# Paired 64 KB loads into a fixed buffer in a memory-bound decode kernel

## The chip, the cores and the metric

The kernel runs on one core of one Trainium2 chip. The metric is device time in microseconds. A difference is called resolved when its 95% interval excludes zero, and "the same" when it stays within 2%.

## The reference, cut to what matters

```
x: [1, 1, 1024]     k_cache, v_cache: [1, 4, 65536, 128]  (67 MB each, bf16)
q = (x @ wq) as 32 heads of 128; each of the 4 KV heads serves 8 query heads
p = softmax(q @ k.T / sqrt(128));  o = p @ v;  a = o @ wo
b = gated MLP of x through w_in [1024, 3584] and w_out [1792, 1024]
out = sigmoid(sum(x * gate_w)) * a + (1 - that) * b
```

One token attends over two caches of 67 MB. With the weights, 162 MB come from HBM and 2 KB go back.

## The kernel before

Every large input goes through one ring of four buffers of 32 KB per partition (a pool with four buffers in turn, called "regions" below where the changed kernel has them in one tile). One sync queue issues all large loads in program order; a load waits until the last reader of its buffer is done.

```python
CT, NKV = 128, 4
def load(src, shape, name):
    t = kv.tile([P, CT * P], BF16, name=name, tag="kv")
    ...
    ins = nc.sync.dma_start(out=v, in_=src)
def load_kv(src, g, j, name):                 # 4 MB: 128 partitions x 32 KB
    k0 = j * CT * P
    return load(src[0, g, k0:k0 + CT * P, :].rearrange("(p c) d -> p (c d)", c=CT),
                (CT * DH,), name)

win_t = [load(... half i of w_in ...) for i in range(2)]
wq_t  = [load(... half i of wq ...) for i in range(2)]
# ... q ...
for g in range(G):                            # 4 KV heads
    for j in range(NT):                       # 4 tiles of 16384 keys
        k_tile(g, j, load_kv(A_k_cache, g, j, "kn"))
        if j == NT - 1:
            stats(g)
        if g > 0:
            v_tile(g - 1, j, load_kv(A_v_cache, g - 1, j, "vt"))
        elif j == NT - 1:
            project(load(... w_out ...), FC, uT, 0, first=True)
    if g > 0:
        head_out(g - 1)
# ... last V tiles, wo in six pieces, then:
nc.scalar.copy(out=out_sb[:], in_=out_ps[:])
nc.scalar.dma_start(out=..., in_=out_sb[::B, :])        # four partitions
```

`k_tile` transposes a K tile on VectorE (DVE) and multiplies it on TensorE (PE); a K buffer is free after its fourth transpose. `v_tile` is PE alone. `stats(g)` is the maximum and the exponentials of head g.

Of the kernel before, what the change touches and what calls it, by code (L numbers as in the profile page):

```python
# [8 lines left out]
BF16 = mybir.dt.bfloat16  # L9
# [5 lines left out]
P = 128  # L15
CT = 128
NKV = 4
B = 32
# [5 lines left out]
WO_SPLIT = ((16,), (8, 4, 2, 1, 1))  # L24
# [3 lines left out]
def kernel(  # L28
# [15 lines left out]
    nc = tc.nc  # L44

    _, _, D = A_x.shape
    _, G, S, DH = A_k_cache.shape
    HD = A_wq.shape[1]
    H = HD // DH
    REP = H // G  # L50
    F = B_w_in.shape[1]
    FH = F // 2
    KC = D // P
    FC = FH // P
    OC = HD // P
    QD = P // H
    NT = S // (P * CT)
# [8 lines left out]
    const = ctx.enter_context(tc.tile_pool(name="const", bufs=1))  # L66
    wk = ctx.enter_context(tc.tile_pool(name="wk", bufs=2))
    big = ctx.enter_context(tc.tile_pool(name="big", bufs=1))
    kv = ctx.enter_context(tc.tile_pool(name="kv", bufs=NKV))
    ktp = ctx.enter_context(tc.tile_pool(name="ktp", bufs=3))  # L70
    scp = ctx.enter_context(tc.tile_pool(name="scp", bufs=NT + 1))
    ptp = ctx.enter_context(tc.tile_pool(name="ptp", bufs=NT + 2))
# [7 lines left out]
    def same_weights(ins):  # L80
        held.add(ins.ins.name)
# [33 lines left out]

    nc.at_finalize(start_first_load)

    def load(src, shape, name):
        t = kv.tile([P, CT * P], BF16, name=name, tag="kv")
        n = 1  # L120
        for s in shape:
            n *= s
        v = t[:, :n]
        if len(shape) == 2:
            v = v.rearrange("p (a b) -> p a b", b=shape[1])
        ins = nc.sync.dma_start(out=v, in_=src)
        if not first_load:
            first_load.append(ins.ins.name)
        return v

    def load_kv(src, g, j, name):
        k0 = j * CT * P
        return load(src[0, g, k0:k0 + CT * P, :].rearrange("(p c) d -> p (c d)", c=CT),
                    (CT * DH,), name)


    xg8 = const.tile([KC, 2, P], BF16, name="xg8")
# [5 lines left out]

    KH = KC // 2
    win_view = B_w_in.rearrange("(p c) n -> p c n", c=KC)
    win_t = [load(win_view[:, i * KH:(i + 1) * KH, :], (KH, F), "win_t") for i in range(2)]
    wq_view = A_wq.rearrange("(p c) n -> p c n", c=KC)
    wq_t = [load(wq_view[:, i * KH:(i + 1) * KH, :], (KH, HD), "wq_t") for i in range(2)]


    row = const.tile([P, P], FP32, name="row")
# [41 lines left out]
    for t in range(2):  # L193
        nc.vector.tensor_tensor(
            out=xm[:, t], in0=xb_ps[:, t * P:(t + 1) * P].rearrange("p (i c) -> p c i", c=KC),
# [51 lines left out]
    for hf in range(2):  # L247
        nc.vector.tensor_tensor(  # L248
            out=zm[:, hf], in0=z_ps[:, hf * HN:hf * HN + ZN].rearrange("p (j c) -> p j c", c=FC),
# [3 lines left out]
                            in_=zm.rearrange("p h j c -> p h c j"), axis=AX.X, op=ALU.add)  # L253
# [44 lines left out]
    for k in range(NHB):  # L298
        xs = slice(k * NX // NHB, (k + 1) * NX // NHB)
        nc.vector.tensor_tensor(  # L300
            out=qm[:, xs], in0=q_ps[:, k * HN:(k + 1) * HN].rearrange("p (x j e) -> p x j e",
                                                                   j=B, e=2),
# [6 lines left out]
        out=q4[:], in0=q1[:].rearrange("p x e -> p (x e)").unsqueeze(1).to_broadcast(  # L309
            [P, NB, NX * 2]),  # L310
# [7 lines left out]
    for g in range(G):  # L318
        k, t0 = g * T2 // NB, g * T2 % NB
        nc.vector.tensor_copy(out=qs[:, g].rearrange("p b (t h) -> p b t h", t=T2),  # L320
                              in_=qv[:, k, t0:t0 + T2].rearrange("p t h b -> p b t h"))

    def build_w(g):
        for v in range(VC):
            nc.vector.tensor_tensor(
                out=wt[g % 2][:, v, :, :, v, :],
                in0=qs[:, g].unsqueeze(2).to_broadcast([P, BP, NB, REP]),
                in1=own_n[:].unsqueeze(1).unsqueeze(3).to_broadcast([P, BP, NB, REP]),
                op=ALU.mult)

    oa = const.tile([P, OC], BF16, name="oa")
# [3 lines left out]
    def k_tile(g, j, kn):  # L335
        kb = kn.bitcast(I32)
        n = CC * DH // 2
        s_ps = pss.tile([P, 2 * HN], FP32, name="s_ps", tag="s")
        for v in range(VC):
            kt = ktp.tile([P, CC * DH], BF16, name="kt")  # L340
            nc.vector.transpose(out=kt[:].bitcast(I32), in_=kb[:, v * n:(v + 1) * n])  # L341
            while late:
                nc.vector.reduce_max(**late.pop())  # L343
            kx = kt[:].rearrange("p (c h k e) -> p h e c k", h=2, k=B, e=2)
            for b in range(BP):
                for k in range(2):
                    ins = nc.tensor.matmul(  # L347
                        s_ps[:, k * HN:(k + 1) * HN],
                        lhsT=wt[g % 2][:, v, b].rearrange("p a v h -> p (a v h)"),
                        rhs=kx[:, b // 2, b % 2, k * CC // 2:(k + 1) * CC // 2, :],  # L350
                        start=(v == 0 and b == 0), stop=(v == VC - 1 and b == BP - 1),
                        skip_group_check=True)
                    if k > 0:
                        same_weights(ins)
        if j == 0:
            mxs[g] = wk.tile([P, NT], FP32, name="mx")
        sct[g, j] = scp.tile([P, CC * B], BF16, name="sc")
        nc.scalar.copy(out=sct[g, j][:], in_=s_ps[:])  # L358
        late.append(dict(out=mxs[g][:, j:j + 1], in_=sct[g, j][:], axis=AX.X))
# [26 lines left out]
    def v_tile(g, j, vt):  # L386
        if j == 0:
            o_ps[g] = pso.tile([P, 2, VC * DH], FP32, name="o_ps")
        vx = vt.rearrange("p (v c d) -> p c v d", v=VC, d=DH)
        for u in range(CC // 2):  # L390
            hs = slice(u % 2 * P // 2, (u % 2 + 1) * P // 2)
            for e in range(2):
                ins = nc.tensor.matmul(  # L393
                    o_ps[g][hs, e, :],
                    lhsT=ptt[g, j][:, 2 * u:2 * u + 2, :].rearrange("p c x -> p (c x)"),
                    rhs=vx[:, 2 * u + e], start=(j == 0 and u < 2),
                    stop=(j == NT - 1 and u >= CC // 2 - 2), skip_group_check=True)
                if e > 0:
                    same_weights(ins)
# [29 lines left out]
    NO = D // NB  # L429
    out_ps = psl.tile([P, NO], FP32, name="out_ps")  # L430

    def project(w, n, vec, c0, first=False, last=False):
        for c in range(n):
            for t in range(NB):
                nc.tensor.matmul(  # L435
                    out_ps[t * B:(t + 1) * B, :],
                    lhsT=vec[:, c0 + c:c0 + c + 1].to_broadcast([P, B]),
                    rhs=w[:, c, t * NO:(t + 1) * NO],
                    start=(first and c == 0), stop=(last and c == n - 1),
                    skip_group_check=True)  # L440
# [2 lines left out]
    build_w(0)  # L443
    for g in range(G):
        for j in range(NT):
            k_tile(g, j, load_kv(A_k_cache, g, j, "kn"))
            if j == 1 and g + 1 < G:
                build_w(g + 1)
            if j == NT - 1:
                stats(g)  # L450
            if g > 0:
                v_tile(g - 1, j, load_kv(A_v_cache, g - 1, j, "vt"))
            elif j == NT - 1:
                project(load(B_w_out.rearrange("(p c) n -> p c n", c=FC), (FC, D), "wout_t"),
                        FC, uT, 0, first=True)
        if g > 0:
            head_out(g - 1)
    for j in range(NT):
        v_tile(G - 1, j, load_kv(A_v_cache, G - 1, j, "vt"))
    head_out(G - 1)  # L460


    wo_view = A_wo.rearrange("(p c) n -> p c n", c=OC)
    c0 = 0
    for split in WO_SPLIT:
        t = kv.tile([P, CT * P], BF16, name="wo_t", tag="kv")
        t = t[:].rearrange("p (c n) -> p c n", n=D)
        b = c0
        for n in split:
            nc.sync.dma_start(out=t[:, c0 - b:c0 - b + n, :], in_=wo_view[:, c0:c0 + n, :])  # L470
            project(t[:, c0 - b:c0 - b + n, :], n, oa, c0, last=(c0 + n == OC))
            c0 += n
    out_sb = const.tile([P, NO], BF16, name="out_sb")
    nc.scalar.copy(out=out_sb[:], in_=out_ps[:])
    nc.scalar.dma_start(out=out.rearrange("o t (q n) -> (o t q) n", n=NO), in_=out_sb[::B, :])

    last = {}
    for ins in list(nc.cur_bb.bb.instructions):
# [36 lines left out]
```

## Time and profile before

| | before |
|---|---|
| time, median | 385.04 us (384.94 to 385.17, 3 runs) |
| span of the profiled run | 383.4 us |
| PE, DVE busy | 62%, 57% |
| load queue's share of 16 DMA engines | 98.6% |

Three lines of the profile's page, of the kernel before: TensorE's busy time, the DMA row of the 40-slice view (9 is 90% or more of a slice), and the load queue's row of the DMA table (packets, MB, share).

```profile
...
PE 237.4 (62%) x1372; PEld 58.5 (15%) x796; DVE 218.3 (57%) x211; ACT 39.6 (10%) x55; POOL 4.4 (1%) x10
...
DMA  9999999999999999999999999999999999999994
...
q1 hardware_dynamic: 6192, 162.01, 98.6%
...
```

Nothing but the DMA engines is full. In the packet records an engine takes packets one after another: their durations add up to 378.1 us per engine, in a window of 378.5 us from the first packet to the last. So the time is first of all the sum of the packets' durations, and then whatever time the queue was empty.

This is the sync queue's timeline of the kernel before around the change from head 0 to head 1 (start, duration, what was issued):

```profile
...
start us, us, engine line op out<-in xcount [idle before <-releaser]
59.26 0.33 SPq L126 DMA_DIRECT2D wout_t<-in_B_w_out_dram  x1
70.54 0.33 SPq L126 DMA_DIRECT2D kn<-in_A_k_cache_dram  x1
81.39 0.33 SPq L126 DMA_DIRECT2D vt<-in_A_v_cache_dram  x1
92.24 0.33 SPq L126 DMA_DIRECT2D kn<-in_A_k_cache_dram  x1
101.17 0.33 SPq L126 DMA_DIRECT2D vt<-in_A_v_cache_dram  x1
...
```

Each load waits for a buffer. The K load at 70.54 reuses K tile 1's buffer, the V load at 81.39 K tile 2's, the K load at 92.24 K tile 3's.

The end of the program, kernel before: the last copy and the output store.

```profile
...
380.47 0.37 ACT L474 CAST out_sb<-out_ps 128x256 bf16<-128x256 f32 x1 [47.63 <-PE out_ps L435]
380.88 0.61 ACTq L475 DMA_DIRECT2D out_dram<-out_sb  x1
```

From the start of the copy to the end of the span (383.375 us) are 2.91 us.

### The profile page before, as it was taken

To read this page: it belongs to the slowest core of one execution; us is meant where nothing else is said; L and a number is where in the kernel's file an instruction comes from. 1 tells how busy PE (TensorE), PEld (TensorE's weight loads), DVE (VectorE), ACT (ScalarE), POOL (GpSimd) and SP (SyncE) were. 2 spreads that over 40 slices of the span, in tenths; PEclk is the share of its full clock that TensorE was granted. 3 is DMA by queue.
4 is the path that set the end of the run, shared out by engine and by line. 5 is a ranking of instruction groups with operands and counts; after the bars stand their busy time and mean duration, and the time that the engine had idled before them with its cause. 6 is when DMAs were issued, how large, how long until landed. Compare 5 with 4: busy or idle time off the path is not lost.

```text
span 383.4 us, 2650 instructions
## 1 busy us (share of the span) xinstructions
PE 237.4 (62%) x1372; PEld 58.5 (15%) x796; DVE 218.3 (57%) x211; ACT 39.6 (10%) x55; POOL 4.4 (1%) x10
## 2 busy tenths in 40 slices
PE   0433357675378749465699393665983937786553
PEld 0110011111212102011121020111210201221132
DVE  4241478996697373758964645679655546720040
ACT  1010001111601101014011010140110101400000
POOL 4000000000000000000000000000000000000000
PEclk9956659999779959698699697975997978668886
DMA  9999999999999999999999999999999999999994
GB/s 374 436 427 427 422 432 431 438 435 437 426 434 424 422 431 434 438 434 431 429 431 427 427 431 433 438 427 427 434 429 424 431 435 434 432 427 428 431 417 193
DMA packets 6248, 162.18 MB, mean 423 GB/s; under 512 B 728, under 2 KB 732, under 8 KB 1116
## 3 DMA queue, kind: packets, MB, share of 16 engines
q1 hardware_dynamic: 6192, 162.01, 98.6%
q8 instruction: 8, 0.13, 0.1%
q14 instruction: 4, 0.03, 0.0%
q10 hardware_dynamic: 44, 0.01, 0.0%
HBM read 162.01 MB, written 0.00 MB: 423 GB/s over the span
## 4 chain that ended last, share of the span: by engine, by line
DMA 63%; DVE 19%; PE 10%; issue 5%; ACT 1%; SPq 0%; ACTq 0%; DVEq 0%
DMA kn<-in_A_k_cache_dram 53%; DVE kt L341 16%; DMA wo_t<-in_A_wo_dram 8%; PE s_ps L347 6%; DMA wb<-in_B_b_sp_dram 3%; PE o_ps L393 3%; DVE pt L383 1%; ACT sc L358 1%; PE z_ps L234 1%; DVE o_sb L408 0%; SPq L470 0%; ACT sc L380 0%; DVE mx L362 0%; DVE om L404 0%; DVE mx L343 0%
## 5 line engine op out<-in xcount | busy, mean ns | idle before, releaser
L347 PE MATMUL s_ps<-kt,wt 128*128 128x512 bf16 x512 | 138.1, 425 | 73.5 <-DVE kt L341 73.4
L341 DVE STREAM_TRANSPOSE kt<-kn 128x2048 int32<-128x2048 int32 x64 | 143.3, 2283 | 68.1 <-DMA kn<-in_A_k_cache_dram 65.2
L393 PE MATMUL o_ps<-vt,pt 128*64 128x512 bf16 x512 | 69.5, 433 | 7.9 <-DMA vt<-in_A_v_cache_dram 7.9
L347 PEld LDWEIGHTS <-wt 128*128 128x128 bf16 x256 | 26.9, 105 | 185.6 <-issue 121.5
L358 ACT CAST sc<-s_ps 128x1024 bf16<-128x1024 f32 x16 | 16.2, 1013 | 254.6 <-PE s_ps L347 254.6
L393 PEld LDWEIGHTS <-pt 128*64 128x64 bf16 x256 | 17.3, 124 | 57.2 <-issue 55.7
L383 DVE STREAM_TRANSPOSE pt<-sc 128x1024 bf16<-128x1024 bf16 x16 | 18.6, 1217 | 6.8 <-ACT sc L380 6.8
L404 DVE TENSOR_TENSOR om<-o_ps,own 128x1024 f32<-128x1024 f32 x4 | 4.8, 1195 | 26.4 <-PE o_ps L393 26.4
L380 ACT ACTIVATE sc<-sc,nb 128x1024 bf16<-128x1024 bf16 x16 | 18.2, 1136 | 9.7 <-DVE nb L376 9.7
L343 DVE TENSOR_REDUCE mx<-sc 128x1 f32<-128x1024 bf16 x12 | 14.3, 1188 | 1.1 <-ACT sc L358 1.0
L362 DVE TENSOR_REDUCE mx<-sc 128x1 f32<-128x1024 bf16 x4 | 4.9, 1220 | 12.1 <-ACT sc L358 12.1
L234 PE MATMUL q_ps<-wq_t,xT 128*32 128x512 bf16 x64 | 7.0, 617 | 7.5 <-DMA wq_t<-in_A_wq_dram 7.5
L414 PE MATMUL om_ps<-o_sb,hsel 128*32 128x128 f32 x8 | 2.1, 353 | 13.9 <-DVE o_sb L408 13.9
L435 PE MATMUL out_ps<-wo_t,oa 128*32 128x256 bf16 x128 | 7.0, 375 | 4.2 <-DMA wo_t<-in_A_wo_dram 2.8
L234 PE MATMUL z_ps<-win_t,xT 128*32 128x448 bf16 x64 | 6.2, 566 | 4.0 <-DMA win_t<-in_B_w_in_dram 4.0
L300 DVE TENSOR_TENSOR rowt<-q_ps,own_b 128x512 f32<-128x512 f32 x2 | 1.3, 686 | 12.4 <-PE q_ps L234 12.4
L408 DVE TENSOR_REDUCE o_sb<-om 128x128 f32<-128x1024 f32 x4 | 7.5, 1872 | 0.1
L366 PE MATMUL mt_ps<-ident_f,m 128*1 128x128 f32 x4 | 1.2, 295 | 10.2 <-DVE m L364 10.2
L248 DVE TENSOR_TENSOR rowt<-z_ps,own_b 128x448 f32<-128x448 f32 x2 | 1.2, 620 | 8.6 <-PE z_ps L234 8.6
L190 PE MATMUL xb_ps<-xg,spread 8*128 8x256 bf16 x1 | 0.4, 365 | 9.1 <-DMA xg<-in_gate_w_dram 9.1
L234 PEld LDWEIGHTS <-xT 128*32 128x32 bf16 x64 | 3.0, 138 | 19.2 <-issue 19.2
L435 PEld LDWEIGHTS <-oa 128*32 128x32 bf16 x128 | 4.5, 126 | 6.8 <-issue 4.1
(88 smaller groups left out, 56.7 us busy)
## 6 DMA issues: line engine op xcount, KB each, us to landing
kn<-in_A_k_cache_dram SPq DMA_DIRECT2D x16, 4096.0 KB, 27.2
vt<-in_A_v_cache_dram SPq DMA_DIRECT2D x16, 4096.0 KB, 32.4
wq_t<-in_A_wq_dram SPq DMA_DIRECT2D x2, 4096.0 KB, 28.2
win_t<-in_B_w_in_dram SPq DMA_DIRECT2D x2, 3584.0 KB, 15.0
wo_t<-in_A_wo_dram SPq DMA_DIRECT2D x1, 4096.0 KB, 25.9
wout_t<-in_B_w_out_dram SPq DMA_DIRECT2D x1, 3584.0 KB
wo_t<-in_A_wo_dram SPq DMA_DIRECT2D x1, 2048.0 KB
wo_t<-in_A_wo_dram SPq DMA_DIRECT2D x1, 1024.0 KB
```

Source lines behind the costliest of these rows:

```text
L234: ins = nc.tensor.matmul(ps[t * B:(t + 1) * B, k * HN:k * HN + n], lhsT=xT[:, i * KH + c:i * KH + c + 1].to_broadcast([P, B]), rhs=w[:, c, ...
L341: nc.vector.transpose(out=kt[:].bitcast(I32), in_=kb[:, v * n:(v + 1) * n])
L343: nc.vector.reduce_max(**late.pop())
L347: ins = nc.tensor.matmul(s_ps[:, k * HN:(k + 1) * HN], lhsT=wt[g % 2][:, v, b].rearrange("p a v h -> p (a v h)"), rhs=kx[:, b // 2, b % 2, ...
L358: nc.scalar.copy(out=sct[g, j][:], in_=s_ps[:])
L362: nc.vector.reduce_max(**late.pop())
L380: nc.scalar.activation(out=sct[g, j][:], in_=sct[g, j][:], func=ACT.Exp, scale=SCALE, bias=nb[:, 0:1], accum_out=lss[g][:, j:j + 1])
L383: nc.vector.transpose(out=ptt[g, j][:].rearrange("p c x -> p (c x)"), in_=sct[g, j][:])
L393: ins = nc.tensor.matmul(o_ps[g][hs, e, :], lhsT=ptt[g, j][:, 2 * u:2 * u + 2, :].rearrange("p c x -> p (c x)"), rhs=vx[:, 2 * u + e], sta ...
L404: nc.vector.tensor_tensor(out=om8[:], in0=o_ps[g][:].rearrange("p e (v d) -> p (e v) d", d=DH), in1=own_8[:].unsqueeze(2).to_broadcast([P, ...
L408: nc.vector.tensor_reduce(out=o_sb[:], in_=om8[:].rearrange("p x d -> p d x"), axis=AX.X, op=ALU.add)
L435: nc.tensor.matmul(out_ps[t * B:(t + 1) * B, :], lhsT=vec[:, c0 + c:c0 + c + 1].to_broadcast([P, B]), rhs=w[:, c, t * NO:(t + 1) * NO], st ...
```

## The change

The intent: larger rows (64 KB per partition) for the V tiles and wq, hence half as many packets; fixed places for all tiles so that two neighbouring regions can take a pair; an output store split over two queues.

```diff
-    kv = ctx.enter_context(tc.tile_pool(name="kv", bufs=NKV))
+    kv = big.tile([P, NKV * CT * P], BF16, name="kv")
-    def load_kv(src, g, j, name):
-        k0 = j * CT * P
-        return load(src[0, g, k0:k0 + CT * P, :].rearrange("(p c) d -> p (c d)", c=CT),
-                    (CT * DH,), name)
+    def load_kv(src, g, j, at, n=1):
+        k0, m = j * CT * P, n * CT
+        v = load(src[0, g, k0:k0 + m * P, :].rearrange("(p c) d -> p (c d)", c=m),
+                 (m * DH,), at)
+        return [v[:, i * CT * DH:(i + 1) * CT * DH] for i in range(n)]
...
-    win_t = [load(..., "win_t") for i in range(2)]
+    win_t = [load(..., 2 + i) for i in range(2)]
-    wq_t = [load(... half i ...) for i in range(2)]
+    wq_a = load(wq_view, (KC, HD), 0)
...
-            k_tile(g, j, load_kv(A_k_cache, g, j, "kn"))
+            k_tile(g, j, load_kv(A_k_cache, g, j, (j + 2) % NKV if g == 0 else j % 2)[0])
...
-            if g > 0:
-                v_tile(g - 1, j, load_kv(A_v_cache, g - 1, j, "vt"))
+            if g > 0 and j % 2 == 1:
+                for i, vt in enumerate(load_kv(A_v_cache, g - 1, j - 1, 2, 2)):
+                    v_tile(g - 1, j - 1 + i, vt)
...  (w_out goes to region 2; the last V tiles are one pair and two singles; wo as before)
-    nc.scalar.dma_start(out=..., in_=out_sb[::B, :])
+    for i, queue in enumerate((nc.scalar, nc.sync)):
+        p0 = (2 * i + 1) * B - 1
+        queue.dma_start(out=out_rows[2 * i:2 * i + 2, :], in_=out_sb[p0:p0 + 2, :])
```

So head 0's K tiles 0 to 3 go to regions 2, 3, 0, 1; from head 1 on, K tiles alternate between regions 0 and 1 and V pairs use regions 2 and 3.

More of the change, by code (lines that the diff above doesn't have):

```diff
@@ L116, with load @@
     nc.at_finalize(start_first_load)
-    def load(src, shape, name):
-        t = kv.tile([P, CT * P], BF16, name=name, tag="kv")
+    kv = big.tile([P, NKV * CT * P], BF16, name="kv")
+    def load(src, shape, at):
         n = 1
@@ L122, in load @@
             n *= s
-        v = t[:, :n]
+        v = kv[:, int(at * CT * P):int(at * CT * P) + n]
         if len(shape) == 2:
@@ L145 @@
     win_view = B_w_in.rearrange("(p c) n -> p c n", c=KC)
-    win_t = [load(win_view[:, i * KH:(i + 1) * KH, :], (KH, F), "win_t") for i in range(2)]
+    win_t = [load(win_view[:, i * KH:(i + 1) * KH, :], (KH, F), 2 + i) for i in range(2)]
     wq_view = A_wq.rearrange("(p c) n -> p c n", c=KC)
-    wq_t = [load(wq_view[:, i * KH:(i + 1) * KH, :], (KH, HD), "wq_t") for i in range(2)]
+    wq_a = load(wq_view, (KC, HD), 0)
+    wq_t = [wq_a[:, i * KH:(i + 1) * KH, :] for i in range(2)]
     row = const.tile([P, P], FP32, name="row")
@@ L450 @@
                 stats(g)
-            if g > 0:
-                v_tile(g - 1, j, load_kv(A_v_cache, g - 1, j, "vt"))
-            elif j == NT - 1:
-                project(load(B_w_out.rearrange("(p c) n -> p c n", c=FC), (FC, D), "wout_t"),
+            if g > 0 and j % 2 == 1:
+                for i, vt in enumerate(load_kv(A_v_cache, g - 1, j - 1, 2, 2)):
+                    v_tile(g - 1, j - 1 + i, vt)
+            elif g == 0 and j == NT - 1:
+                project(load(B_w_out.rearrange("(p c) n -> p c n", c=FC), (FC, D), 2),
                         FC, uT, 0, first=True)
@@ L457 @@
             head_out(g - 1)
-    for j in range(NT):
-        v_tile(G - 1, j, load_kv(A_v_cache, G - 1, j, "vt"))
+    for j, n, at in ((0, 2, 0), (2, 1, 2), (3, 1, 3)):
+        for i, vt in enumerate(load_kv(A_v_cache, G - 1, j, at, n)):
+            v_tile(G - 1, j + i, vt)
     head_out(G - 1)
@@ L464 @@
     c0 = 0
-    for split in WO_SPLIT:
-        t = kv.tile([P, CT * P], BF16, name="wo_t", tag="kv")
-        t = t[:].rearrange("p (c n) -> p c n", n=D)
-        b = c0
+    for at, split in enumerate(WO_SPLIT):
         for n in split:
-            nc.sync.dma_start(out=t[:, c0 - b:c0 - b + n, :], in_=wo_view[:, c0:c0 + n, :])
-            project(t[:, c0 - b:c0 - b + n, :], n, oa, c0, last=(c0 + n == OC))
+            t = load(wo_view[:, c0:c0 + n, :], (n, D), at + c0 % (OC // 2) * D / (CT * P))
+            project(t, n, oa, c0, last=(c0 + n == OC))
             c0 += n
     out_sb = const.tile([P, NO], BF16, name="out_sb")
+    out_rows = out.rearrange("o t (q n) -> (o t q) n", n=NO)
     nc.scalar.copy(out=out_sb[:], in_=out_ps[:])
-    nc.scalar.dma_start(out=out.rearrange("o t (q n) -> (o t q) n", n=NO), in_=out_sb[::B, :])
+    for i, queue in enumerate((nc.scalar, nc.sync)):
+        p0 = (2 * i + 1) * B - 1
+        queue.dma_start(out=out_rows[2 * i:2 * i + 2, :], in_=out_sb[p0:p0 + 2, :])
     last = {}
```

## The prediction

> **What bounds the kernel now.** The DMA engines. The DMA table gives the load queue 98.6% of 16 engines over the 383.4 us span; the 40-slice row of DMA shows 9 in every slice but the last; PE is busy 62%, DVE 57%. In the trace's DMA packet records the load queue runs 378.5 us from first to last packet, with the engines idle about 1 us of it on average. The other 5 us are 1 us before the first packet and the last projection, copy and output store. So the time is the sum of packet times per engine; compute matters only if it lets the queue run dry.
>
> **Cost of a packet.** From the records (median ns): 2 KB 84, 4 KB 162, 8 KB 313, 16 KB 614, 32 KB 1216. The last step is 602 ns for 16 KB, so a packet costs about 12 ns plus 36.7 ns per KB. A 32 KB packet runs at 16 x 32768 B / 1216 ns = 431 GB/s. The Trainium skill, "DMA: Bandwidth & Descriptors", section "Where 436 GB/s comes from", puts the ceiling at 435.2 GB/s; the trace agrees, and leaves about 1% to win by packet size.
>
> **What the change does.**
> 1. V (7 pairs, 56 MB) and wq (8 MB) go from 32 to 64 KB per partition. If a row becomes one packet, each engine has 64 fewer: estimate 64 x 12 ns = 0.77 us, packet 2.42 us. Eight fewer DMAs save eight semaphore packets of 9 ns per engine, 0.07 us; if rows are cut back to 32 KB, only this remains. All of it is on the critical path. The wider row pitch should do no harm: wq already has it, at about 1216 ns a packet.
> 2. Fixed regions and pairs shift when buffers come free. The queue is already full, so this costs only if it drains. Tightest is the start: wq lands whole at about 39.1 us rather than half at 29.4, so its two matmul groups (3.4 and 3.6 us) run in series, q is ready at about 50.8 rather than 47.3, and the first K transpose starts 0.5 us later than its 50.34. Head 1's first K load then waits for K tile 2 (freed 81.4, estimate 81.9; queue dry at about 88), the next for K tile 3 (92.2 to 92.7; dry at 98), the V pair for the B projection (101.2 to 101.7; dry at 107.6). At least 5 us to spare. Later a V pair waits for two V tiles (PE 4.3 us each) with two K tiles, 19.5 us, queued behind: about 10 us to spare. No new stall.
> 3. Output: one store of four partitions becomes two of two. The store's wait of 2.5 us is nearly all latency (packets 31 to 34 ns). The Trainium skill, same page, section "Issuing engines are not separate DMA queues", says that only issue time (here 0.3 us) can be saved: 0.1 us either way.
>
> **Predicted: 384.2 us, range 383.6 to 384.9 (8 in 10). Faster by over 2%: 0.01; within 2%: 0.97; slower: 0.02.**
>
> **What would show it.** Right: 65536-byte packets of about 2.42 us; load queue window 0.6 to 1.0 us shorter; first K transpose near 50.8 us; no slice of the DMA row below 9 before the last. Wrong: 32 KB packets still; 64 KB packets of over 2.43 us; idle DMA engines near 82 to 108 us.
>
> **What would make it wrong.** Dependency tracking of one big tile could serialise loads against readers of other regions (tens of us slower); 64 KB rows could meet slower HBM access; the program's end could change by more; drift between chips of 0.2 us would be a quarter of the effect.

## More of the kernel before

The completion marks in the trace's DMA records (one small packet for each engine and DMA) show that w_out lands between 85.5 and 87.5 us, the K load of 70.54 between 95.2 and 97.3, and the V load of 81.39 between 104.9 and 107.0. At 92.24 there are thus still two loads ahead of the new one, and it could have come some 12 us later. The ranges have a width of 2 us because the sixteen engines do not keep step.

Busy time in stretches of that part (stretch; its length; engines; granted clock, DMA share, GB/s). A packet counts whole in the stretch in which it starts, so a share can be above 1, and a share or a rate of a single 5 us stretch is only a rough sign.

```profile
...
core 0: us, PE busy (x) PEld busy (x) DVE busy (x) ACT busy (x) POOL busy (x), PEclk, DMA share, GB/s
...
94.00:99.00 5.00, 1.74 (x22) 1.19 (x24) 2.03 (x5) 1.50 (x2) 0.00 (x0) 0.83 0.99 426
99.00:104.00 5.00, 2.12 (x44) 1.39 (x36) 2.91 (x3) 4.99 (x8) 0.00 (x0) 0.83 1.04 442
104.00:109.00 5.00, 0.94 (x3) 0.25 (x2) 5.00 (x4) 0.45 (x2) 0.00 (x0) 0.52 1.04 446
...
```

## The result, and the profile after

Ratios here and below are the mean time of one kernel's fast runs over that of the kernel before in the same rounds, so not quite the ratio of the medians that are quoted.

| | before | after |
|---|---|---|
| median, first runs | 385.08 us (384.94 to 385.17, 6 runs) | 384.62 us (384.36 to 385.90, 6 runs) |
| ratio, 95% interval | | 0.9994 (0.998 to 1.0008) |
| span of the profiled run | 383.4 us | 383.9 us |
| load queue, packets | 6192 | 5044 |
| first load packet to last completion mark | 378.5 us | 379.3 us |
| mean time of load packets per engine | 378.11 us | 377.57 us |

The last two rows are worked out from the trace's DMA packet records: the first as end less start, the second as the sum of all load packets' durations over 16. The median lies in the predicted range, but no gain is resolved, and single times scatter over 1.5 us where before's scatter over 0.2 us. The profiled execution of the changed kernel was its slowest one, 385.90 us; that made visible what the median hides.

The same three lines of the page, kernel after:

```profile
...
PE 235.8 (61%) x1372; PEld 60.3 (16%) x796; DVE 218.7 (57%) x211; ACT 39.6 (10%) x55; POOL 4.4 (1%) x10
...
DMA  9999999999999999999999999999999999999994
...
q1 hardware_dynamic: 5044, 162.01, 98.4%
...
```

The packets fell by 1148: 1024 fewer rows (8192 KB x 8 DMAs, 128 rows each), 128 fewer completion marks (8 DMAs x 16), and 4 more for the half of the output that now leaves on this queue. The rows did become single 64 KB packets, of 2421 ns at the median. The engines' mean work fell, yet the last engine was done later. The row of nines does not show why: its slices are 9.6 us wide.

The sync queue's timeline, kernel after, answers the one shown before:

```profile
...
59.00 0.33 SPq L126 DMA_DIRECT2D kv<-in_B_w_out_dram  x1
82.45 11.18 SPq L126 DMA_DIRECT2D kv<-in_A_k_cache_dram  x2
102.46 0.33 SPq L126 DMA_DIRECT2D kv<-in_A_v_cache_dram  x1
...
```

The line at 82.45 merges two K loads. The same timeline with a shorter window gives the second by itself:

```profile
...
93.30 0.33 SPq L126 DMA_DIRECT2D kv<-in_A_k_cache_dram  x1
```

Head 1's first K load now waits for K tile 2 (82.45 us, not 70.54), its second for K tile 3 (93.30). The first lands between 95.1 us on the fastest engine and 96.9 on the slowest (completion marks). So the second was issued 1.8 us before the fastest engines ran out. That was too late: in the packet records several engines start the new load without a pause at 95.1 to 95.3 us, but others take their next packet only at 96.1 to 96.6.

Busy time in stretches, kernel after, the same columns as before:

```profile
...
94.00:99.00 5.00, 1.74 (x9) 0.53 (x5) 1.87 (x4) 1.01 (x1) 0.00 (x0) 0.92 0.96 387
99.00:104.00 5.00, 3.41 (x58) 2.25 (x57) 2.01 (x3) 4.41 (x6) 0.00 (x0) 0.50 1.06 449
104.00:109.00 5.00, 0.00 (x0) 0.00 (x0) 5.00 (x5) 1.51 (x4) 0.00 (x0) 0.50 1.13 472
...
```

From 94 to 99 us the DMA share falls to 0.96 and the rate to 387 GB/s, against 0.99 and 426 before. The packet records are the firmer evidence. On top of the idle time, packets are stretched when the queue starts again, as they are at the program's start. Counting packets over 60 ns above the median of their size: 21 of them start between 96 and 102 us, 4973 ns in sum, and another 8 between 104 and 106 us, 2895 ns, after the V pair that was issued at 102.46 us (2.5 us before the fastest engine was done with the load before it at 105.0). In before there is one such packet in all of 94 to 110 us, at 102.8 us, just as a 16 KB instruction fetch of 1.1 us ends. The sixteen engines lose 209 ns idle on average at 95 to 97 us, and (4973 + 2895) / 16 = 492 ns in stretched packets: about 0.7 us, which is most of the 0.84 us that the larger rows were to bring. Some engines lose more than that, and the program ends with the slowest: its completion marks lie 1.8 us behind the fastest engine's ahead of this stretch and 3.4 us behind after it, while the other fifteen stay within 1.8 us. In before they lie 2.1 us apart on both sides. How much of that one engine's delay is the stall's is not shown: an instruction fetch of 1.0 us at 102.2 us, with a packet stretched by 0.5 us right behind it, also falls in this stretch.

The end of the program, kernel after:

```profile
...
381.28 0.37 ACT L476 CAST out_sb<-out_ps 128x256 bf16<-128x256 f32 x1 [55.41 <-PE out_ps L437]
381.68 0.33 SPq L479 DMA_DIRECT2D out_dram<-out_sb  x1
381.68 0.26 ACTq L479 DMA_DIRECT2D out_dram<-out_sb  x1
```

From the start of the copy to the end of the span are 2.62 us, 0.29 us less than before. The store's issue shrank from 0.61 us to 0.33 and 0.26 side by side.

### The profile page after: what moved, and what is told of

It is laid out like the page before. It is cut to its first block, busy times and chain, and to the rows that moved or that the text cites. A ratio compares the mean times of both kernels' runs of the same rounds, so it can differ in the third digit from the quotient of the medians.

```text
span 383.9 us, 2639 instructions
## 1 busy us (share of the span) xinstructions
PE 235.8 (61%) x1372; PEld 60.3 (16%) x796; DVE 218.7 (57%) x211; ACT 39.6 (10%) x55; POOL 4.4 (1%) x10
## 3 DMA queue, kind: packets, MB, share of 16 engines
q1 hardware_dynamic: 5044, 162.01, 98.4%
## 4 chain that ended last, share of the span: by engine, by line
DMA 57%; PE 20%; DVE 16%; issue 4%; ACT 2%; SPq 0%; ACTq 0%; DVEq 0%
DMA kv<-in_A_v_cache_dram 31%; DMA kv<-in_A_k_cache_dram 16%; DVE kt L343 13%; PE o_ps L395 11%; PE s_ps L349 8%; DMA kv<-in_A_wo_dram 7%; DMA wb<-in_B_b_sp_dram 3%; DVE pt L385 1%; PE z_ps L236 1%; ACT sc L360 1%; DVE o_sb L410 0%; SPq L126 0%; ACT L382 0%; ACT sc L382 0%; DVE om L406 0%
## 5 line engine op out<-in xcount | busy, mean ns | idle before, releaser
L343 DVE STREAM_TRANSPOSE kt<-kv 128x2048 int32<-128x2048 int32 x64 | 142.7, 2280 | 40.7 <-DMA kv<-in_A_k_cache_dram 40.7
L395 PE MATMUL o_ps<-kv,pt 128*64 128x512 bf16 x512 | 66.6, 425 | 21.9 <-DMA kv<-in_A_v_cache_dram 21.9
L395 PEld LDWEIGHTS <-pt 128*64 128x64 bf16 x256 | 18.8, 122 | 67.5 <-issue 61.4
L236 PE MATMUL q_ps<-kv,xT 128*32 128x512 bf16 x64 | 5.9, 546 | 10.8 <-DMA kv<-in_A_wq_dram 10.8
L437 PE MATMUL out_ps<-kv,oa 128*32 128x256 bf16 x128 | 7.0, 376 | 4.2 <-DMA kv<-in_A_wo_dram 2.8
L236 PE MATMUL z_ps<-kv,xT 128*32 128x448 bf16 x64 | 6.4, 576 | 3.8 <-DMA kv<-in_B_w_in_dram 3.8
```

The source lines that it names most:

```text
L236: ins = nc.tensor.matmul(ps[t * B:(t + 1) * B, k * HN:k * HN + n], lhsT=xT[:, i * KH + c:i * KH + c + 1].to_broadcast([P, B]), rhs=w[:, c, ...
L343: nc.vector.transpose(out=kt[:].bitcast(I32), in_=kb[:, v * n:(v + 1) * n])
L395: ins = nc.tensor.matmul(o_ps[g][hs, e, :], lhsT=ptt[g, j][:, 2 * u:2 * u + 2, :].rearrange("p c x -> p (c x)"), rhs=vx[:, 2 * u + e], sta ...
L437: nc.tensor.matmul(out_ps[t * B:(t + 1) * B, :], lhsT=vec[:, c0 + c:c0 + c + 1].to_broadcast([P, B]), rhs=w[:, c, t * NO:(t + 1) * NO], st ...
```

## The experiments

All outputs are right. "After" is the changed kernel.

The theory: the 64 KB rows pay what their packets save, about 0.8 us, and the new order of regions takes it back by letting the queue run nearly dry around 95 and 104 us. Rivals: the slow runs are chance (instruction fetches that fall on one engine); or packet size is worth nothing.

### after_again: the changed kernel, more runs

No edit.

> The changed kernel unaltered, with more rounds, as the yardstick of this chip. If its first timing was typical: 0.3 to 0.7 us below the kernel before, single times scattered over more than 1 us, and the load queue again briefly idle between 94 and 99 us. If the 0.77 us of fewer packets arrived in full and the slow profiled run was a chance event: 0.8 to 1.1 us below before, scatter as small as before's 0.2 us.

Measured: 385.61 us median (384.80 to 386.45, 5 runs) against 385.12; ratio 1.0006 (0.9993 to 1.0019). The scatter is real, and with it the changed kernel gains nothing. The profile shows the same place: 21 packets stretched by 9262 ns in sum between 94 and 100 us, 13 by 4682 ns between 104 and 108. The expected gain of 0.3 to 0.7 us was a miss: these runs were slower than the first six.

### out_only: before, with the split output store alone

```diff
-    nc.scalar.dma_start(out=..., in_=out_sb[::B, :])
+    for i, queue in enumerate((nc.scalar, nc.sync)):
+        p0 = (2 * i + 1) * B - 1
+        queue.dma_start(out=out_rows[2 * i:2 * i + 2, :], in_=out_sb[p0:p0 + 2, :])
```

> The kernel before with only the split output store. Theory A (the prediction): 0.1 us either way, not resolved. Theory B, from the two profiles (last copy's start to end of span 2.91 us before, 2.62 us after): faster by about 0.3 us, 384.8 us, and the same 2.6 us in its own profile.

Measured: 384.97 us median (384.72 to 385.21), ratio 0.9996 (0.9984 to 1.0008): 0.15 us, not resolved. The end of its timeline:

```profile
...
380.33 0.37 ACT L474 CAST out_sb<-out_ps 128x256 bf16<-128x256 f32 x1 [47.82 <-PE out_ps L435]
380.73 0.32 SPq L478 DMA_DIRECT2D out_dram<-out_sb  x1
380.73 0.25 ACTq L478 DMA_DIRECT2D out_dram<-out_sb  x1
```

The span ends at 383.0 us, so copy to end is about 2.7 us. The saving of 0.2 to 0.3 us is seen in the two profiles' ends and is about what the store's issue shrank by; the timing is too coarse to confirm it.

### cut_rows: after, each 64 KB row cut into two packets by holes

```diff
-    kv = big.tile([P, NKV * CT * P], BF16, name="kv")
+    PITCH = CT * P + 16                      # 32 bytes between regions
+    kv = big.tile([P, NKV * PITCH], BF16, name="kv")
...      a pair is still one DMA, but its destination has a hole, so a row is two packets
```

> The changed kernel with a 32 byte hole between the regions, so that each 64 KB row leaves as two 32 KB packets of the same DMA: same DMAs, same waits, same order. Packet theory: slower than the changed kernel by 64 packets of 12 ns, 0.6 to 0.9 us, so at or above the kernel before; packets of 65536 B gone. Rival (the gain is the output store and the packets are worth nothing): same as the changed kernel within 0.2 us. The near-dry queue at 95 us stays in both.

Measured: 386.99 us median (384.41 to 387.54, 6 runs), ratio 1.0036 (1.0015 to 1.0057). Slower, as the packet theory says, but by 1.4 us rather than 0.6 to 0.9, and with a scatter of 3 us that makes the number useless: the near-dry queue is still in it. Its profiled run (385.72 us) was not one of the slow ones, so what happened at 387 us stays open. The test had to be repeated without the stall.

### early_slot: after, with an earlier free region for head 1

```diff
-            k_tile(g, j, load_kv(A_k_cache, g, j, (j + 2) % NKV if g == 0 else j % 2)[0])
+            k_tile(g, j, load_kv(A_k_cache, g, j, (2, 0, 1, 3)[j] if g == 0 else j % 2)[0])
```

Head 1's K loads into regions 0 and 1 now wait for K tiles 1 and 2.

> The changed kernel with the four K tiles of head 0 in regions 2, 0, 1, 3 instead of 2, 3, 0, 1, so that head 1's first two K loads wait for K tiles 1 and 2 (about 70 and 82 us) and not 2 and 3 (82 and 93 us). Stall theory: the idle DMA engines and stretched packets at 94 to 99 us go, 0.3 to 0.8 us faster than the changed kernel, and single times scatter less. Rival (the profiled run was slow by chance, instruction fetches falling on one DMA engine): no difference, scatter stays.

Measured: 384.36 us median (384.20 to 385.02), ratio 0.9986 (0.9974 to 0.9998), and 1.25 us below the changed kernel in the same rounds, more than the 0.3 to 0.8 expected. The sync queue's timeline:

```profile
...
70.61 11.94 SPq L126 DMA_DIRECT2D kv<-in_A_k_cache_dram  x2
102.23 0.33 SPq L126 DMA_DIRECT2D kv<-in_A_v_cache_dram  x1
...
```

No packet is stretched between 94 and 102 us any more. Between 104 and 106 five still are, by 3184 ns in sum: the V pair is still issued at 102.23 us, and the fastest engine finishes the load before it at 104.7 us. A lead of 2.5 us is too little. The scatter (0.8 us) shrank, but did not go.

### early_slot_proj and early_slot_proj2: the second near-dry place mended too

The V pair waits for w_out's region, and the B projection that reads it stood behind the statistics of head 0 in PE's order. It is moved ahead of them.

```diff
  # against early_slot
+            if g == 0 and j == NT - 1:
+                project(load(B_w_out..., (FC, D), 2), FC, uT, 0, first=True)
             if j == NT - 1:
                 stats(g)
...
-            elif g == 0 and j == NT - 1:
-                project(load(B_w_out..., (FC, D), 2), FC, uT, 0, first=True)
```

> early_slot, and the B projection is emitted before the softmax statistics of head 0, so that the first V pair, which waits for it, is issued near 98 us and not 102.2. Stall theory: the slow 64 KB packets that remain at 104 to 106 us (3184 ns in sum over the engines in early_slot) go; 0.1 to 0.6 us faster than early_slot, 383.8 to 384.2 us, scatter of single times under 0.6 us. Rival (chance placement of instruction fetches): same as early_slot within 0.1 us.

Measured: 384.31 us median, ratio 0.998 (0.9967 to 0.9994), just above the expected 383.8 to 384.2. One run, the profiled one, took 482.52 us: PE was slow, as two lines of its page show (PE's busy time, and the K matmuls at 671 ns against 425 in before). Why is not shown: the record lists a granted clock of 1.0 for this run, so it does not show a throttle. It is left out.

```profile
...
PE 391.9 (82%) x1372; PEld 72.6 (15%) x796; DVE 219.9 (46%) x211; ACT 39.6 (8%) x55; POOL 4.4 (1%) x10
...
L349 PE MATMUL s_ps<-kt,wt 128*128 128x512 bf16 x512 | 239.9, 671 | 28.2 <-DVE kt L343 28.2
...
```

The same kernel was run again as a yardstick for the last experiments:

> early_slot_proj again, unaltered, since its one profile fell in the slow state and as yardstick for the three beside it. 384.2 to 384.5 us; in a fast profile no packet stretched between 94 and 106 us beyond the single ones of instruction fetches.

Measured: 384.49 us median (384.27 to 384.58), ratio 0.9981 (0.9969 to 0.9994). The sync queue's timeline and the stretches:

```profile
...
70.27 11.18 SPq L126 DMA_DIRECT2D kv<-in_A_k_cache_dram  x2
95.58 0.33 SPq L126 DMA_DIRECT2D kv<-in_A_v_cache_dram  x1
...
```

```profile
...
94.00:99.00 5.00, 2.15 (x59) 1.60 (x51) 2.03 (x5) 1.89 (x2) 0.00 (x0) 1.00 1.07 455
99.00:104.00 5.00, 0.00 (x0) 0.00 (x0) 3.39 (x3) 4.96 (x9) 0.00 (x0) 0.65 1.00 426
104.00:109.00 5.00, 1.41 (x4) 0.40 (x3) 5.00 (x4) 0.00 (x0) 0.00 (x0) 0.50 1.02 439
...
```

The V pair is issued at 95.58 us, 9 us ahead. The dip at 94 to 99 us is gone, and so are the stretched packets (one remains, at 99.1 us, right behind an instruction fetch, as in before at 102.8). The scatter is 0.3 us, near before's. The gain over before is 0.66 us and resolved. The step from early_slot to this kernel, however, is not resolved in the median: 0.76 us below before there and 0.81 and 0.66 here. They were run at other times. What it visibly removes is the scatter. Instruction fetches by themselves do not make the scatter: the profiles of before, after, after_again, early_slot and this kernel all have one of 16 KB between 98 and 104 us, and the kernels without a near-dry place scatter by 0.2 to 0.6 us all the same. Whether a fetch on an engine that is already late adds to a slow run was not separated.

### late_slot: a large dose of the same stall

```diff
-            (j + 2) % NKV if g == 0 else j % 2
+            (2, 3, 1, 0)[j] if g == 0 else j % 2
```

> The changed kernel with head 0's K tiles in regions 2, 3, 1, 0, so that head 1's first K load waits for K tile 3 (freed at 93 us) and not K tile 2 (82 us): a large dose of the same stall. Stall theory: queue dry from 85.4 (fast engines) to 87.2 us (slow ones) until about 95 us, the load queue's share between 84 and 96 us falls to about a quarter, and 8 to 10 us are lost in full: 393 to 395 us. Rival (the queue has slack elsewhere to make up): well under 8 us.

Measured: 393.03 us median (392.03 to 394.57, 4 runs), ratio 1.021 (1.0186 to 1.0234): 7.9 us slower than before, 7.4 slower than the changed kernel. It was run at another time. The issue at the critical place (two K loads at once), and the stretches:

```profile
...
91.72 0.80 SPq L126 DMA_DIRECT2D kv<-in_A_k_cache_dram  x2
...
```

```profile
...
84.00:94.00 10.00, 6.68 (x29) 1.24 (x13) 7.69 (x4) 0.32 (x1) 0.00 (x0) 1.00 0.31 107
94.00:99.00 5.00, 2.10 (x31) 1.58 (x35) 2.03 (x5) 1.67 (x2) 0.00 (x0) 0.73 0.97 419
...
```

The issue came at 91.7 us, a little earlier than I expected. The engines ran dry from 85.4 to 87.3 us and took the first new packets at 92.7 to 93.4, 1.0 us and more after the start of the issue; the DMA share between 84 and 94 us is 0.31. In the packet records the engines stand empty for 7.1 us on average between 84 and 94 us, and 9060 / 16 = 0.57 us of stretched packets come on top: 7.7 us. The kernel to compare with is early_slot_proj, which has the change without the stall: against its 384.31 us the profiled run (392.25 us) lost 7.9 us and the median 8.7. So nothing was made up later. Against before the loss is just under the expected 8 to 10 us, against early_slot_proj just within. What the slower runs lost beyond 7.9 us, the one profile cannot say.

### early_slot_proj_cut: rows cut by holes, without the stall

The edit of cut_rows on top of early_slot_proj.

> early_slot_proj with each 64 KB row cut into two 32 KB packets of the same DMA (32 byte hole between regions): the clean test of packet size, without a near-dry queue to blur it. Packet theory: 64 packets more per engine of 12 ns, 0.77 us (0.5 to 1.0) slower than early_slot_proj. Rival (packet size is worth nothing, the rest of the gain is the output store and fewer DMAs): within 0.2 us of early_slot_proj.

Measured: 384.23 us median (384.15 to 384.33), ratio 0.9977 (0.9964 to 0.9991). Not slower at all. Taken alone this refutes the packet theory. The packet records say otherwise: the holes had a second effect. Mean packet in ns, without those that are more than 40 ns off the usual value, for the K tiles of head 2 in this one profile:

| K tile | region | moved by holes | mean packet |
|---|---|---|---|
| 0 | 0 | 0 bytes | 1218.1 |
| 1 | 1 | 32 bytes | 1213.3 |
| 2 | 0 | 0 bytes | 1218.1 |
| 3 | 1 | 32 bytes | 1213.2 |

Packets into region 1, which a hole had moved, were 5 ns shorter, so the holes also made packets cheaper. That does not hold for every moved packet: of the V pair that lands between 182.6 and 202.0 us, in regions moved by 64 and 96 bytes, the packets of about the first third took 1213 ns and those after 191 us about 1217. Over the whole run the 280 packets of 32 KB per engine average 1215.4 ns, 2.2 ns below the kernel before, which gives back some 0.6 us. Two controls were needed: a cut without holes, and a shift without a cut.

### two_rows: rows cut, nothing moved

```diff
  # against early_slot_proj: a V pair is one DMA of two rows of 32 KB per partition
-        k0, m = j * CT * P, n * CT
-        v = load(src[0, g, k0:k0 + m * P, :].rearrange("(p c) d -> p (c d)", c=m), (m * DH,), at)
+        k0 = j * CT * P
+        s = src[0, g, k0:k0 + n * CT * P, :].rearrange("(r p c) d -> p r (c d)", r=n, c=CT)
+        v = kv[:, at * CT * P:(at + n) * CT * P]
+        nc.sync.dma_start(out=v.rearrange("p (r x) -> p r x", r=n), in_=s)
```

> early_slot_proj with each V pair loaded by the same single DMA but as two 32 KB rows per partition, taken from the two tiles' own places in memory; the destination has no holes, so nothing is shifted in on-chip memory. Packet theory: 56 packets more per engine at 12 to 13 ns, 0.67 to 0.73 us slower than early_slot_proj, so about 385.0 us; packets of the K and V tiles 1218 ns on clean average as in the kernel before. Rival (early_slot_proj_cut lost nothing because packet size is worth nothing): within 0.2 us of early_slot_proj.

Measured: 385.13 us median (385.02 to 385.28), ratio 0.9998 (0.9985 to 1.0012), and 0.64 us slower than early_slot_proj2 in the same rounds; the two sets of times do not overlap. The packets: 1217.8 ns here, against 2422.0 ns for one of 64 KB, so a 64 KB packet saves 2 x 1217.8 - 2422.0 = 13.6 ns, and 56 of them 0.76 us per engine. The packet theory holds. (wq is still one 64 KB row in this kernel; its V pairs hold the same keys as the K tiles.)

### keys_matched: the right keys beside the right weights

```diff
  # against early_slot_proj
+    def load_k(g, j, at):
+        if g == G - 1 and j >= 2:                       # these V tiles are single
+            return load_kv(A_k_cache, g, j, at)[0]
+        k0 = (j - j % 2) * CT * P
+        s = A_k_cache[0, g, k0:k0 + 2 * CT * P, :].rearrange("(p r c) d -> p r (c d)", r=2, c=CT)
+        return load(s[:, j % 2], (CT * DH,), at)
```

> early_slot_proj with the K tiles of a pair read in rows of 32 KB at a 64 KB pitch, so that each partition holds the same keys as the V pair's rows, which the changed kernel does not keep. It should cost nothing: within 0.2 us of early_slot_proj. If a 64 KB source pitch of 32 KB rows is slower, K packets would be over 1218 ns on clean average.

Measured: 384.55 us median (384.40 to 384.63), ratio 0.9983 (0.9971 to 0.9996), 0.06 us from early_slot_proj2. K packets average 1217.6 ns in both. Mending the order of keys is free.

### keys_matched_shift: all regions moved by 32 bytes

```diff
  # against keys_matched
-    kv = big.tile([P, NKV * CT * P], BF16, name="kv")
+    kv = big.tile([P, 16 + NKV * CT * P], BF16, name="kv")
-        v = kv[:, int(at * CT * P):int(at * CT * P) + n]
+        v = kv[:, 16 + int(at * CT * P):16 + int(at * CT * P) + n]
```

> keys_matched with all four regions moved up by 32 bytes. In early_slot_proj_cut, packets into regions that a hole had moved were 2 to 4 ns shorter (1213 to 1216 against 1218). If the shift of the destination does it: clean averages of 1213 to 1215 and 2416 to 2419 ns and 0.5 to 1.0 us faster than keys_matched, 383.4 to 383.8 us. If it was the phase between engines or the holes between neighbouring tiles: no difference, 1218 and 2422.

Measured: 382.95 us median (382.72 to 383.27), ratio 0.9943 (0.993 to 0.9955): 1.60 us below keys_matched, more than I expected. 32 KB packets average 1213.0 ns, 64 KB packets 2418.0, with 99% of the 32 KB packets at exactly 1213. This is the fastest version.

### before_shift: the shift without the change

```diff
  # against before: the same four buffers in the same turn, from one tile
-    kv = ctx.enter_context(tc.tile_pool(name="kv", bufs=NKV))
+    kv = big.tile([P, 16 + NKV * CT * P], BF16, name="kv")
+    turn = [0]
+    def region():
+        a = 16 + turn[0] % NKV * CT * P
+        turn[0] += 1
+        return kv[:, a:a + CT * P]
```

> The kernel before, its four buffers taken in the same turn from one tile and moved up by 32 bytes; no pairs, old output store. If the place of the destination alone shortens packets: nearly every 32 KB packet 1213 ns (clean average 1218 before), 272 packets per engine at about 4.7 ns, 1.3 us faster than before, 383.6 to 384.0 us. Rival (the shift pays only beside 64 KB rows or the new buffer order): 1218 ns and within 0.2 us of before.

Measured: 383.28 us median (383.14 to 383.36), ratio 0.9952 (0.9939 to 0.9966). Moving the buffers of the kernel before by 32 bytes, with nothing else of the change, gives 1.8 us (1.3 were expected), more than everything that the change intended. That the 32 bytes do it, and not the change from four buffers to one tile, is seen from keys_matched and keys_matched_shift, which differ in that shift alone. On the shifted buffers the mended change is worth 0.33 us in the medians (keys_matched_shift against this kernel, in different calls), less than the 0.6 us on unshifted ones. The packets agree with that: on shifted buffers a 64 KB packet saves only 2 x 1213.0 - 2418.0 = 8.0 ns and not 13.6, and the work of the table below falls by 0.62 us (376.61 to 375.99) and not by 0.95 (378.11 to 377.16).

Packets and ends of all kernels in one table, worked out from the DMA records of their profiled runs (mean packets as above; "work" is the sum of load packets over 16; "last mark" is the end of the last load's last completion mark, counted from the span's start):

| kernel | 32 KB, ns | 64 KB, ns | work, us | last mark, us | median time, us |
|---|---|---|---|---|---|
| before | 1217.6 | | 378.11 | 379.49 | 385.08 |
| after | 1217.0 | 2421.3 | 377.57 | 380.37 | 384.62 |
| after_again | 1217.0 | 2421.3 | 377.80 | 380.81 | 385.61 |
| early_slot | 1217.4 | 2421.8 | 377.23 | 379.55 | 384.36 |
| early_slot_proj2 | 1217.6 | 2422.0 | 377.11 | 378.81 | 384.49 |
| two_rows | 1217.8 | 2418.1 (wq) | 377.90 | 379.39 | 385.13 |
| keys_matched | 1217.6 | 2422.0 | 377.16 | 378.89 | 384.55 |
| keys_matched_shift | 1213.0 | 2418.0 | 375.99 | 377.35 | 382.95 |
| before_shift | 1213.0 | | 376.61 | 377.72 | 383.28 |

## Why the prediction was right or wrong

- **What bounds the kernel** was right. late_slot shows the converse: time for which the queue is empty is lost in full.
- **The cost of a packet** was right. 12 ns per packet was an estimate from the step between 16 and 32 KB; 64 KB packets appeared at 2421 ns (2.42 us predicted), and two_rows puts the saving at 13.6 ns a packet and 0.64 us in time, against 0.67 us estimated for V's 56. Only the shifted kernels show that this saving depends on the buffers' place (8.0 ns there).
- **"At least 5 us to spare ... No new stall" was the step that failed.** For the second K load of head 1 I put the release at 92.7 us and "dry at 98". The release was right (93.30). The dry time was wrong: I had counted from the moment when a waiting reader saw a load, which is the slowest engine's landing, while the fastest engine of the sixteen ran out at 95.1 us. And I allowed no time between the issue and the first packet, which on an empty queue was 1.0 us (late_slot), while four engines that had run out at 95.3 to 95.7 us took their first packet of the load issued at 93.30 only at 96.1 to 96.6. So not 5 us were to spare but less than none. The next step, the V pair, had 2.5 us and not 5.9. The cause is not the late wq that I discussed. The first K transpose, shown below from DVE's timeline of the kernel after, began at 50.09 us, not 50.8: both q groups together took 5.9 us and not the 7.0 that I added up, so DVE was done with q at 49.48 us and then waited 0.61 us for the K load, as it waited for it in before (3.10 us, to 50.34). The cause is the map of regions. In the kernel before, head 1's first K load waits for K tile 1 and a V load for K tile 2; the second K load waits for K tile 3 as well, but it has that V load ahead of it in the queue. In the changed kernel the two K loads come first and wait for K tiles 2 and 3.

```profile
...
48.59 0.89 DVE L327 TENSOR_TENSOR wt<-qs,own_n 128x128 bf16<-128x128 bf16 x4
50.09 6.70 DVE L343 STREAM_TRANSPOSE kt<-kv 128x2048 int32<-128x2048 int32 x3 [0.61 <-DMA kv<-in_A_k_cache_dram]
```

The last line's counterpart in the kernel before:

```profile
...
50.34 6.70 DVE L341 STREAM_TRANSPOSE kt<-kn 128x2048 int32<-128x2048 int32 x3 [3.10 <-DMA kn<-in_A_k_cache_dram]
...
```

- **The size** fell with that step. The load queue's window was to shrink by 0.6 to 1.0 us and grew from 378.5 to 379.3 in the profiled run. 384.2 us was predicted; the first median of 384.62 lies in the range, the second of 385.61 does not, and in neither is a gain resolved. With the two near-dry places removed the gain came: 0.66 us (early_slot_proj2), of the 0.84 predicted for packets and marks. The record's list of runs shows where the rest went: the span between first and last instruction did shrink by 0.9 us (median 383.3 in before, 382.4 in early_slot_proj2), but the time outside the span, which is 1.8 us in before, out_only and before_shift, averages 2.0 to 2.15 us in every kernel with the pairs. What fills it stays open. The right range was partly luck: a gain and a loss of like size stood side by side.
- **The output store**: 0.1 us either way was predicted. The ends of the profiles show 0.2 to 0.3 us saved, and the timing cannot tell. The Trainium skill ("DMA: Bandwidth & Descriptors", section "Issuing engines are not separate DMA queues") has it that a second queue saves only issue time, and that agrees: the issue took 0.61 us before (I had taken it for 0.3) and 0.33 beside 0.26 after.
- **What I listed as a danger** did not occur: one big tile does not serialise its regions, and 64 KB rows meet no slower memory.
- **What I did not think of**: the V pairs change which keys stand beside which weights; and the place of the buffers matters more than the packet size.

What stays open: why 32 bytes matter (the packets of wq took 1213 ns in the kernel before too, at an unmoved destination, so the place is not the whole of it); which other shifts do as well; what the 0.2 to 0.3 us outside the span are; and why cut_rows scattered by 3 us.

## What to carry to other kernels

When a queue is always full, count for every load how long before the *fastest* engine runs out it is issued, and keep several microseconds: here 9 us was safe and 2.5 us was not, although no slice of the profile's DMA row showed it. A fixed map of buffers is a schedule, so list for each load whose release it waits for before and after. Look at single packets' durations when a kernel runs at the DMA engines' limit: here a place that made them 0.4% shorter made the kernel 0.5% faster; and test a reordering of keys or rows with inputs on which the order matters.

## What the Trainium skill lacked or had wrong

- "DMA: Bandwidth & Descriptors", section "Where 436 GB/s comes from": it says that for transfers from HBM the HBM side, about 358 GB/s, binds. Here one core's loads averaged 423 GB/s over the whole span, near the 435.2 GB/s that the same section gives for the other side. The section derives the 358 GB/s as half of what two cores share, so what does not hold is that it binds one core alone. (The page's own table of single-core loads, with the pair's other core idle, at 425 GB/s for 16 MB, agrees with the run.)
- The same page, section "Latency and other measured facts": about 0.6 us to the first byte. That agrees when it is counted from the end of the issue instruction: in late_slot the issue ran from 91.72 to 92.05 us, and the first packet on the empty queue started at 92.7. What the page lacks is a lead to plan with: here a lead of 1.8 us left four engines idle, and one of 2.5 us still gave stretched packets.
- The same page has costs per packet for small transfers only. The runs show 13.6 ns saved for each 64 KB packet in place of two of 32 KB, 0.64 us in 385, and 8.0 ns on the shifted buffers.
- "SBUF — State Buffer", section "Operand start alignment", says of itself that it is about legality, not speed, and no page has the effect of a 32 byte shift of the destination on a large DMA's rate (the DMA page counts transactions by a start's distance from 256 B; no run here relates the two). Here 32 bytes made 32 KB packets 1213.0 ns in place of 1217.6 and the kernel before 1.8 us faster.
- No page gives a size for how far apart the engines that share one DMA can stand: the completion marks of one load spread over 2.1 us in before and 3.4 us in after.
